# A new hand-written order for the start of a fused scan and feed-forward kernel

## The chip, the cores and the metric

The kernel runs on one core of one Trainium2 chip. The metric is the device time of one execution in microseconds. The median of three runs before the change is 116.46 us (116.0 to 116.67).

## What is computed

A state-space scan over x (4 batches, 8 heads, 768 steps, 32 channels) in chunks of 32 steps, with decays a and the projections B and C, is followed by a feed-forward layer with a squared ReLU.

```python
for c in range(nc):                                  # chunks of 32 steps
    cum = np.cumsum(la, axis=-1)                     # la = log(a)
    L = np.exp(cum[:, :, :, None] - cum[:, :, None, :]) * causal
    CB = np.einsum('bhin,bhjn->bhij', Cc, Bc)
    y_intra = np.einsum('bhij,bhjd->bhid', CB * L, xc)
    y_inter = np.einsum('bhin,bhnd->bhid', Cc, state) * decay_to_i
    y[:, :, sl] = y_intra + y_inter
    state = decay_full * state + np.sum(Bx, axis=2)  # Bx = B x, decayed to the chunk's end
...
h = np.maximum(x @ w_in, 0.0)                        # x: 3072 tokens of 256; w_in: 256 x 2048
out = (h * h @ w_out)                                # w_out: 2048 x 256
```

## The kernel before

The scan is cut into 12 units (`UNITS`: 4 batches by 3 thirds of 256 steps, the first third of all batches first). Each unit yields one block of 256 tokens for the feed-forward layer, so there are 12 blocks, a to l. TensorE does all products, ScalarE and VectorE take results out of PSUM, GpSimd prepares operands and issues the weight loads, SP issues most other loads.

Nothing is scheduled by the compiler: the string `ORDER` lists every step by a short name, and the loop over it emits the instructions of each step. Each engine then runs its own instructions in that order and waits at an instruction until what it needs is there. So the place of a name in the string sets the order on each engine and on each DMA queue.

The names, for unit or block k:

- `fa0`, `fa1`, `la`: loads of a (the two halves for the first third of the steps, then the rest); `ldC`, `ldB`, `ldx`: loads of a unit (`:l`/`:h` halves; the last letter is the queue: `a` ScalarE, `s` SP); `ld4` all three.
- `gB2`, `gB3`: a GpSimd memset of one column of the buffer that a load will fill, so that the load waits for GpSimd to get there (L134).
- `wi0` to `wi3`, `wo0` to `wo3`: loads of a quarter of w_in (L139) and of w_out (L143), issued by GpSimd, cast to bf16 on the way.
- `id3:512`: three matmuls on a constant (L476) that compute nothing that is used.
- `sk`, `sp`, `pk`, `su`, `to`, `fq`, `ps`, `iv`: the running product of a (L468, L469), its transposition by TensorE (L452), the totals (Ptot, L524) and their reciprocals and spread copies (Pinv, Pquad, P_sb). `sn`, `p2`, `pq`: the same for the later steps.
- `pc`, `pb`, `px`: C times the decay, the cast of B (both into jt), x over the decay (xs); `tr` and `tc`: transposition of jt by TensorE (L195) and the copy into bct. From unit 4 on the transposition is a DMA.
- `mt`: 16 matmuls that put a unit's scores into PSUM banks 0 to 3 (L220); `mk`: VectorE masks one bank straight from PSUM (L229, 0.68 us); `sc` with `ms`: ScalarE copies the bank out (L234) and VectorE or GpSimd masks the copy (L238).
- `u`: the unit's state update (16 matmuls); `sf`: the state times Pquad (Sd, L343); `in`, or its halves `ina` and `inb`: masked scores times xs (L245); `ca`: the carried state's part; `t`: the copy of the unit's result into T; `us`: the copy of its state out of PSUM.
- `a0` to `a7` (and so on to `l7`): up-projection of block a, eight parts, each four matmuls into one PSUM bank (L403) and a ReLU on ScalarE (L408); `qa0`: the square on VectorE (L414); `A0` to `A7`: the down-projection of that part, four matmuls that accumulate (L430).

Of the eight PSUM banks one is taken per up-projection in turn (`bank()`), from those that are not in use at that place of the order; a bank is free again where its reader stands in the order. A matmul into a bank waits for the bank's last reader. At most eight transfers of the ScalarE and SP queues are under way at a time: each waits for the one eight before it.

From `D0` on the order is a regular mixture of up- and down-projections, with the next units' steps between them.

Of the kernel before, what the change touches and what calls it, by code (L numbers as in the profile page):

```python
# [30 lines left out]
def kernel(  # L31
# [13 lines left out]
    nc = tc.nc  # L45
# [18 lines left out]
        g7 qg6 G3 mk8 h0 qg7 G4 pc10 pb10 px10 ld11 h1 qh0 G5 mk8 h2 qh1 G6 h3 qh2 G7 rg9 za9 zb9 sa9 sb9 h4 qh3 H0
        mk9 tr10 h5 qh4 H1 mk9 h6 qh5 H2 h7 qh6 H3 mk9 i0 qh7 H4 pc11 pb11 px11 i1 qi0 H5 mk9 i2 qi1 H6 i3 qi2 H7
        rg10 za10 zb10 sa10 sb10 i4 qi3 I0 mk10 tr11 i5 qi4 I1 mk10 i6 qi5 I2 i7 qi6 I3 mk10 j0 qi7 I4 j1 qj0 I5 mk10
        j2 qj1 I6 j3 qj2 I7 rg11 za11 zb11 sa11 sb11 j4 qj3 J0 mk11 j5 qj4 J1 mk11 j6 qj5 J2 j7 qj6 J3 mk11 k0 qj7 J4
        k1 qk0 J5 mk11 k2 qk1 J6 k3 qk2 J7 rg12 k4 qk3 K0 k5 qk4 K1 k6 qk5 K2 k7 qk6 K3 l0 qk7 K4 l1 ql0 K5 l2 ql1 K6
        l3 ql2 K7 l4 ql3 L0 l5 ql4 L1 l6 ql5 L2 l7 ql6 L3 ql7"""
# [694 lines left out]
```

## Time and profile before

| | |
|---|---|
| median of three runs | 116.46 us |
| the profiled execution | 116.84 us |
| its span, first to last instruction | 115.1 us |
| TensorE busy (matmuls) | 108.9 us |
| VectorE, ScalarE, GpSimd busy | 84.2, 76.7, 49.8 us |
| moved by DMA | 13.46 MB, 117 GB/s over the span |

The rows that the prediction shows come from these views. The first part of the page gives busy time, share and number of instructions of each engine. The chain that ended last is followed back from the last instruction, and its line gives each engine's share of it. A row of the costliest groups reads: line, engine, operation, what is written and read, sizes, count; then the total busy time, the mean of one in ns; then the idle time of that engine just before, and what ended it. A row of the timeline reads: start, duration, engine, line, operation, and in brackets the idle time before it and what ended it; rows with a count merge equal instructions that follow each other. A row of the windows reads: stretch, its length, then busy time of PE, PEld (weight loads), DVE (VectorE), ACT (ScalarE), POOL (GpSimd) with counts, the granted clock, the share of the DMA engines and GB/s. A row of the DMA issues ends with the size and the time from issue to landing.

### The profile page before, as it was taken

The numbers are of one execution on the slowest core, as the hardware profiler recorded it, in microseconds if no ns is written. First come the engines' busy times: TensorE is split into PE (matmuls) and PEld (weight loads), VectorE is DVE, ScalarE is ACT, GpSimd is POOL, SyncE is SP. The second block draws the span as 40 slices with busy tenths as digits, with TensorE's granted clock in tenths as the row PEclk, the third lists the DMA queues.
The fourth block names the chain that finished last, engine by engine and source line by source line (L and its number), as shares of the span: only waits on it lengthen the run. The fifth ranks groups of instructions, "written<-read, shape, count | busy, mean of one in ns | idle before, by whom it ended". The sixth has DMA issues, their size and how long they took to land.

```text
span 115.1 us, 3998 instructions
## 1 busy us (share of the span) xinstructions
PE 108.9 (95%) x1623; PEld 93.5 (81%) x1623; DVE 84.2 (73%) x187; ACT 76.7 (67%) x161; POOL 49.8 (43%) x102
## 2 busy tenths in 40 slices
PE   7977969999999999999999999999999999999990
PEld 2344749978898989989989989989989899899980
DVE  2469996779599969969965989849668488445530
ACT  0655667865598756787486686786777776876840
POOL 7369972068599457548602669038020020000000
PEclk9999999999999999999999999999999999999999
DMA  1999999989999913935915926623023020020202
GB/s 29 199 196 145 199 203 189 215 167 210 180 191 211 214 24 108 160 89 155 179 46 122 178 97 123 132 95 73 0 100 68 0 100 0 6 91 0 91 0 91
DMA packets 47814, 13.46 MB, mean 117 GB/s; under 512 B 44276, under 2 KB 45876, under 8 KB 47796
## 3 DMA queue, kind: packets, MB, share of 16 engines
q1 hardware_dynamic: 43828, 10.64, 44.8%
q0 software_dynamic: 1664, 2.10, 10.8%
q10 hardware_dynamic: 2304, 0.48, 2.0%
q8 instruction: 12, 0.20, 0.8%
q14 instruction: 6, 0.05, 0.1%
HBM read 10.58 MB, written 3.15 MB: 119 GB/s over the span
## 4 chain that ended last, share of the span: by engine, by line
PE 87%; DMA 6%; POOL 2%; issue 1%; DVE 1%; ACT 1%; ACTq 0%; DVEq 0%
PE pp L430 36%; PE pp L403 36%; PE pp L245 6%; DMA w_out_b<-in_moe_w_out_dram 6%; PE pp L476 4%; PE pp L220 3%; POOL mts L238 1%; PE pp L195 1%; POOL jt L158 1%; PE pp L452 1%; DVE jt L158 0%; DVE Sd L343 0%; ACT bct L208 0%; PE pp L521 0%; ACT osl L722 0%
## 5 line engine op out<-in xcount | busy, mean ns | idle before, releaser
L408 ACT ACTIVATE hb<-pp 128x512 bf16<-128x512 f32 x96 | 55.0, 599 | 24.7 <-PE pp L403 23.1
L430 PE MATMUL pp<-w_out_b,h 128*128 128x256 bf16 (+1 forms) x400 | 54.3, 268 | 0.8 <-DMA w_out_b<-in_moe_w_out_dram 0.8
L414 DVE TENSOR_TENSOR h<-hb 128x512 bf16<-128x512 bf16 x96 | 45.0, 486 | 12.7 <-ACT hb L408 12.3
L403 PE MATMUL pp<-T,w_in_b 128*128 128x256 bf16 x384 | 54.2, 273 | 0.0
L403 PEld LDWEIGHTS <-w_in_b 128*128 128x128 bf16 x384 | 41.4, 114 | 2.2 <-issue 1.0
L430 PEld LDWEIGHTS <-h 128*128 128x128 bf16 x400 | 37.6, 98 | 5.4 <-DVE T L210 1.1
L229 DVE TENSOR_TENSOR mts<-pp,mask 128x512 bf16<-128x512 f32 x45 | 29.6, 677 | 3.3 <-PE pp L220 3.3
L331 POOL TENSOR_TENSOR Sd<-z,Pquad 128x256 bf16<-128x256 f32 x16 | 11.1, 693 | 32.9 <-DVE z L315 25.7
L177 POOL TENSOR_TENSOR xs<-x_nat,Pinv 128x256 bf16<-128x256 f32 (+1 forms) x19 | 14.4, 776 | 5.2 <-DVE Pinv L546 4.6
L158 POOL TENSOR_TENSOR jt<-C_nat,P_sb 128x128 bf16<-128x128 f32 x22 | 9.4, 449 | 1.5 <-ACT P_sb L688 1.0
L476 PE MATMUL pp<-const-bfloat16-1.0 128*128 128x512 bf16 (+2 forms) x19 | 7.3, 516 | 0.8 <-PEq L748 0.8
L315 DVE SCALAR_TENSOR_TENSOR z<-z,Ptot,us 128x64 f32<-128x64 f32 x8 | 2.2, 281 | 6.3 <-ACT us L299 5.4
L437 ACT COPY osb<-pp 128x512 f32<-128x512 f32 x11 | 6.3, 584 | 0.4 <-PE pp L430 0.4
L245 PE MATMUL pp<-mts,xs 64*32 64x128 bf16 x384 | 5.9, 219 | 0.1
L170 POOL CAST jt<-B_nat 128x128 bf16<-128x128 f32 x17 | 5.4, 341 | 1.4 <-DMA B_nat<-in_B_dram 1.4
L220 PE MATMUL pp<-bct 32*64 32x256 bf16 x192 | 5.1, 279 | 0.9 <-DVE bct L210 0.6
L476 PEld LDWEIGHTS <-const-bfloat16-1.0 128*128 128x128 bf16 x19 | 2.2, 122 | 4.0 <-issue 3.7
L245 PEld LDWEIGHTS <-xs 64*32 64x32 bf16 x384 | 4.2, 90 | 0.6 <-issue 0.4
L282 ACT CAST T<-pp 128x512 bf16<-128x512 f32 x7 | 4.1, 592 | 0.4 <-PE pp L245 0.2
L208 ACT CAST T<-pp 128x256 bf16<-128x256 f32 x8 | 2.6, 375 | 2.6 <-PE pp L245 2.6
L245 PE MATMUL pp<-bct,Sd 128*128 128x128 bf16 x40 | 4.2, 220 | 0.0
L220 PEld LDWEIGHTS <-bct 32*64 32x64 bf16 x192 | 2.1, 102 | 2.0 <-issue 0.6
(62 smaller groups left out, 53.4 us busy)
## 6 DMA issues: line engine op xcount, KB each, us to landing
x_nat<-in_x_dram SPq DMA_DIRECT2D x11, 256.0 KB, 3.7
out_dram<-osb SPq DMA_DIRECT2D x11, 256.0 KB, 3.2
B_nat<-in_B_dram SPq DMA_DIRECT2D x11, 128.0 KB, 3.1
C_nat<-in_C_dram SPq DMA_DIRECT2D x11, 128.0 KB, 3.4
w_in_b<-in_moe_w_in_dram POOLq DMA_DIRECT2D x4, 256.0 KB, 6.8
w_out_b<-in_moe_w_out_dram POOLq DMA_DIRECT2D x4, 256.0 KB, 8.2
x_nat<-in_x_dram ACTq DMA_DIRECT2D x2, 128.0 KB, 3.4
bct<-jt SPq DMA_TRANSPOSE x8, 3.6
```

The lines of the kernel that those rows point to most:

```text
L158: eng.tensor_tensor(out=_fap(jt[k % 3], 128 + 144 * g, [[384, 2], [32, 4], [1, 16]]), in0=_fap(loaded[k]["C"], 128 * g, [[16, 2], [32, 4], ...
L177: eng.tensor_tensor(out=_fap(xs, 256 * r, [[256, 2 // n], [32, 8], [1, 32]]), in0=_fap(loaded[k]["x"], 32 * r, [[32, 2 // n], [64, 8], [1, ...
L220: nc.tensor.matmul(pp[64 * u:64 * u + 64, q, r * 256:r * 256 + 256], bct[32 * q:32 * q + 32, r, 0, u * 64:u * 64 + 64], _fap(bct[32 * q:32 ...
L229: nc.vector.tensor_tensor(out=live[k]["mts"][:, q].rearrange("p r g i -> p (r g i)"), in0=pp[:, q, :], in1=mask, op=ALU.mult)
L245: nc.tensor.matmul(dst, w, v, start=bool(need), stop=False, skip_group_check=True, **({} if pos is None else {"tile_position": pos}))
L331: nc.gpsimd.tensor_tensor(out=_fap(S_d, 0, [[128, 2], [32, 4], [1, 32]]), in0=_fap(z, 0, [[32, 2], [0, 4], [1, 32]]), in1=_fap(Pquad, 4 * ...
L403: nc.tensor.matmul(pp[:, h, i * 256:(i + 1) * 256], _fap(w, g * w.shape[2] + (o // 2) * 512 + 2 * (o % 2) + i, [[4, 128]]), T[blk][:, g].r ...
L408: nc.scalar.activation(out=hb.rearrange("p i t -> p (i t)"), in_=pp[:, h, :], func=AF.Relu)
L414: nc.vector.tensor_tensor(out=h2, in0=hb, in1=hb, op=ALU.mult)
L430: nc.tensor.matmul(dst, h2[:, i, r * 128:(r + 1) * 128], w_out_b[gi][:, 2 * o + i, c0:c1], start=first, stop=(fp == 7 and i == 1), skip_gr ...
L437: nc.scalar.copy(out=osb, in_=pp[:, 6 if blk == 1 else 7, :])
L476: nc.tensor.matmul(pp[:, h, 0:int(cols)], ones_b[:, 0:128], ones_b[:, 0:int(cols)] if dep is None else dep, start=True, stop=True, skip_gr ...
```

## The change

The first third of `ORDER` is rewritten up to `D0`, and from there it stays as it was. The pieces are the same but for these: GpSimd's first work is the constants that the start needs, then Pquad (`fq`), then one weight load after the other, with a mask (`ms0`), the scaling of unit 1's x (`px1`) and another mask (`ms1`) among them, and the gate of unit 2's B after the third w_in. Both halves of a are the first transfer of their queue, then come C, B and x of unit 0, then C, B and x of unit 1, then the rest of a. Some fillers go (19 matmuls become 18, eleven before the first product become six). Three quarters of unit 0's and unit 1's scores are masked straight from PSUM. C of unit 0 and of unit 1 is scaled on VectorE, half of unit 0's B is cast there, and one T half of units 0 and 1 is copied there. The state scaling of units 0 and 1 moves from VectorE to ScalarE, as four instructions. The up-projection `a0` stands ahead of the second scores `mt1`, and the down-projections of block a start before unit 1 is finished; blocks a, b and c follow in turn, each down-projection soon after its square. The totals for the later steps (`sn`, `p2`, `pq`) come some 50 names later.

```diff
     ORDER = """
-        id3:512 fa1:a la fa0:s ku ef ldx0:h:a eb id2:512 ti id1:512 gB3 pi ldB0:l:a hd ldC0:l:a ldB0:h:s ldC0:h:s
-        ldx0:l:a wm jz0:v mb jz1:v ldB1:s id3:512 sk pbh0:a id2:512 pk pbl0:p wi0 sp pc0:v ldC1:s trB0 wi1 su iv1:0:8
-        trC0 tcC0:0:v tcB0:2:a id1:512 tcC0:1:a ps pb1:a to px0:v jz2:v mt0 id1:512 u0:67 ldx1:s pc1:p fq sc0 mk0
-        id1:512 mk0 ms0:p tr1 tc1:1:v sc0 tc1:0:a sf0 mt1 ldB2:s wo0 ldC2:s ms0:v ldx2:s id1:384 in0 ca0 iv:8:16
-        id3:512 px1:p t0:aa id1:256 mk1 a0 a1 mk1 mk1 mk1 u1 ina1 inb1 sn1 us0 sf1 qa0 a3 ldC3:s wi2 fr p2 wi3 ca1
-        qa1 wo1 pc2 pb2:a t1:vv us1 iv:32:64 a2 zb0 qa2 zb1 A0 ldB3:s wo2 ldx3:s b3 qb3 b0 pq b2 b1 tr2 wo3 sb1 qa3
-        qb0 A1 b5 b4 qb1 qb2 qb5 tc2:1:v qb4 tc2:0:a a5 B0 b6 B1 a7 qa5 iv:16:32 px2 a6 mt2 B3 A2 sc2 u2 b7 us2 pb3:a
-        pc3 mk2 qa6 px3 mk2 A5 ms2:v mk2 ld4 qb6 sf2 a4 qa7 B5 pc4 A6 A3 ld5 pb4 ina2 inb2 tr4 ca2 t2:aa tr3 B4 B2
-        tc3:0:a tc3:1:a u3:45 qb7 ld6 ld7 mt3 qa4 B6 mk3 mk3 mk3 mk3 us3 c4 c5 c0 A4 A7 B7 c6 qc0 za3 qc4 c1 qc5 qc6
-        sa3 px4 qc1 pc5 pb5 bk c2 rg4 tr5 C0 mk4 mk4 qc2 c7 qc7 sb0 c3 qc3 d2 d1 C5 za4 afC2 d0 C1 px5 C4 qd2 zb3 C6
-        C3 qd0 d3 C2 mk4 mk4 C7 px6 sa4 rg5 qd3 sb3 pc6 zb4 sb4 pb6 D0 d4 qd1 tr6 mk5 za5 zb5 sa5 sb5 D1 iv:64:96 mk5
+        id3:512 fa1:a fa0:s ef jz0:v ldC0:l:a ldC0:h:s eb id2:512 ldB0:l:a ldB0:h:s hd ti ldx0:l:s ldx0:h:s ku pi
+        id1:512 sk wm mb jz1:v ldC1:s ldB1:s ldx1:s la sp id1:512 pk id1:256 pc0:v iv1:0:8 trC0 pbh0:a pbl0:v id1:384
+        tcC0:0:v tcC0:1:a trB0 su tcB0:2:a ps px0:v iv:8:16 to mt0 fr fq wi0 u0:67 id3:512 sc0 mk0 mk0 ms0:p sf0:a
+        mk0 pb1:a id1:512:0 ca0 ina0 id1:512 inb0 wo0 pc1:v t0:av px1:p id1:512 tr1 tc1:1:v tc1:0:a us0 id1:512 wi1
+        a0 mt1 mk1 sc1 mk1 a1 wo1 u1 qa0 ms1:p id2:512 ina1 mk1 A0 sf1:a qa1 inb1 ca1 t1:av A1 wi2 us1 iv:16:32 b0
+        gB2 ldC2:s ldB2:s ldx2:s wo2 jz2:v zb0 zb1 b1 a2 qb0 wi3 a3 qb1 wo3 B0 qa2 b2 B1 qa3 b3 qb2 A2 qb3 A3 sn1 B2
+        sb1 B3 a4 b4 qa4 a5 qb4 pc2 pb2:a gB3 ldC3:s ldB3:s ldx3:s ld4 ld5 b5 qa5 A4 qb5 tr2 tc2:1:v tc2:0:a B4 px2
+        p2 pq A5 iv:32:64 B5 a6 mt2 sc2 u2 us2 b6 mk2 qa6 mk2 a7 mk2 ms2:v qb6 sf2 b7 qa7 A6 qb7 ina2 inb2 B6 ca2
+        t2:aa pc3 pb3:a px3 pc4 pb4 tr4 A7 B7 c0 c1 qc0 tr3 tc3:0:a tc3:1:a c2 qc1 c3 qc2 u3:45 mt3 C0 mk3 qc3 C1 mk3
+        C2 mk3 us3 C3 mk3 za3 sa3 bk c4 c5 qc4 C4 px4 pc5 pb5 ld6 tr5 ld7 c6 qc5 C5 c7 qc6 rg4 mk4 C6 qc7 sb0 mk4 C7
+        zb3 sb3 za4 d0 sa4 px5 d1 mk4 qd0 d2 mk4 qd1 d3 px6 rg5 qd2 qd3 pc6 zb4 sb4 pb6 D0 d4 tr6 mk5 za5 zb5 sa5 sb5
+        D1 iv:64:96 mk5 d5 qd4 D2 pb7 d6 qd5 d7 qd6 D3 zb2 e0 qd7 mk5 e1 qe0 sb2 D4 mk5 D5 ld8 pc7 e2 qe1 D6 e3 qe2
...
-    def ph_sd_first(k):
+    def ph_sd_first(k, eng=None):
...
+        if eng is nc.scalar:
+            for q in range(4):
+                nc.scalar.activation(out=_fap(S_d, 32 * q, [[128, 2], [1, 32]]),
+                                     in_=_fap(pp, v["h"][0] * 512 + 256, [[32, 2], [1, 32]]),
+                                     func=AF.Copy, scale=Pquad[:, total(0, b, 0), q:q + 1])
+            v["S"] = [None, S_d]
+            return
```

More of the change, by code (lines that the diff above doesn't have):

```diff
@@ L64 @@
[L64 to L68, printed above, removed]
@@ L697, in one @@
                 "ms": lambda: mask_copied(k, eng),
-                "u": lambda: first_u(k, f[1] if len(f) > 1 else None), "sf": lambda: ph_sd_first(k),
+                "u": lambda: first_u(k, f[1] if len(f) > 1 else None), "sf": lambda: ph_sd_first(k, eng),
                 "ca": lambda: ph_carry(k, live[k]["h"], live[k]["begun"]),
```

14 lines of the change are left out of this document (9 added, 5 removed).

## The prediction

> **What bounds the kernel now.** I read the page first: busy shares, the chain that ended last, the costliest groups.
>
> ```profile
> span 115.1 us, 3998 instructions
> ...
> PE 108.9 (95%) x1623; PEld 93.5 (81%) x1623; DVE 84.2 (73%) x187; ACT 76.7 (67%) x161; POOL 49.8 (43%) x102
> ...
> PE 87%; DMA 6%; POOL 2%; issue 1%; DVE 1%; ACT 1%; ACTq 0%; DVEq 0%
> ...
> L408 ACT ACTIVATE hb<-pp 128x512 bf16<-128x512 f32 x96 | 55.0, 599 | 24.7 <-PE pp L403 23.1
> ...
> L414 DVE TENSOR_TENSOR h<-hb 128x512 bf16<-128x512 bf16 x96 | 45.0, 486 | 12.7 <-ACT hb L408 12.3
> L403 PE MATMUL pp<-T,w_in_b 128*128 128x256 bf16 x384 | 54.2, 273 | 0.0
> ...
> L229 DVE TENSOR_TENSOR mts<-pp,mask 128x512 bf16<-128x512 f32 x45 | 29.6, 677 | 3.3 <-PE pp L220 3.3
> L331 POOL TENSOR_TENSOR Sd<-z,Pquad 128x256 bf16<-128x256 f32 x16 | 11.1, 693 | 32.9 <-DVE z L315 25.7
> L177 POOL TENSOR_TENSOR xs<-x_nat,Pinv 128x256 bf16<-128x256 f32 (+1 forms) x19 | 14.4, 776 | 5.2 <-DVE Pinv L546 4.6
> ```
>
> TensorE carries 87% of the chain; once its stream is dense, only a stop of TensorE moves the end. So I read its timeline for where the stream starts and stops, and then the windows with the stops.
>
> ```profile
> 0.85 4.85 PE L476 MATMUL pp<-const-bfloat16-1.0 128*128 128x512 bf16 x11 [0.85 <-PEq L748]
> 5.63 0.64 PE L452 MATMUL pp<-eye_f,cp 64*64 64x32 f32 x8
> ...
> 8.09 0.42 PE L220 MATMUL pp<-bct 32*64 32x256 bf16 x16 [0.24 <-ACT bct L208]
> ...
> 11.44 0.93 PE L476 MATMUL pp<-const-bfloat16-1.0 128*128 128x512 bf16 x4
> 12.20 1.03 PE L403 MATMUL pp<-T,w_in_b 128*128 128x256 bf16 x8
> ...
> 16.96 0.60 PE L430 MATMUL pp<-w_out_b,h 128*128 128x256 bf16 x4 [0.81 <-DMA w_out_b<-in_moe_w_out_dram]
> 17.39 1.91 PE L403 MATMUL pp<-T,w_in_b 128*128 128x256 bf16 x16
> ```
>
> ```profile
> 14.00:15.00 1.00, 0.82 (x12) 0.49 (x10) 0.96 (x3) 0.61 (x2) 0.98 (x4) 1.00 1.05 195
> 15.00:16.00 1.00, 0.91 (x8) 0.76 (x8) 1.00 (x5) 0.54 (x5) 0.76 (x2) 1.00 1.22 215
> 16.00:17.00 1.00, 0.19 (x3) 0.07 (x2) 1.00 (x4) 0.53 (x4) 0.73 (x2) 1.00 1.22 198
> ...
> 26.00:28.00 2.00, 1.89 (x22) 1.56 (x25) 2.00 (x4) 1.33 (x5) 1.77 (x3) 1.00 1.09 209
> ```
>
> The stream of useful work begins with a0 at 12.20. After that the windows show 0.18 + 0.09 + 0.81 + 0.11 = 1.2 us of idle in four stops, and none worth counting later. Sixteen matmuls lie 1.91 us from first start to last end while one lasts 0.273, so they start 0.109 apart and each record runs 0.16 beyond the next possible start: a stop costs its idle plus 0.16, and the four cost 1.8 us. A group of four (one a0, one A0) is 0.44.
>
> **The start.** Here are the rows that set it.
>
> ```profile
> a_nat<-in_a_dram ACTq DMA_DIRECT2D x1, 16.0 KB, 1.6
> ...
> B_nat<-in_B_dram SPq DMA_DIRECT2D x1, 64.0 KB, 3.1
> ...
> a_nat<-in_a_dram SPq DMA_DIRECT2D x1, 16.0 KB, 3.0
> ```
>
> ```profile
> 4.68 0.22 DVE L468 TENSOR_SCALAR a_cl<-a_nat 64x128 f32<-64x128 f32 x1 [0.99 <-DMA a_nat<-in_a_dram]
> ...
> 11.00 2.42 DVE L229 TENSOR_TENSOR mts<-pp,mask 128x512 bf16<-128x512 f32 x4
> ...
> 18.72 1.14 DVE L414 TENSOR_TENSOR h<-hb 128x512 bf16<-128x512 bf16 x3 [0.57 <-ACT hb L408]
> ```
>
> ```profile
> 8.44 0.18 ACT L524 COPY Ptot<-pp 128x8 f32<-128x8 f32 x1
> ...
> 11.43 0.65 ACT L208 CAST T<-pp 128x256 bf16<-128x256 f32 x2 [1.41 <-PE pp L245]
> ...
> 13.81 0.28 ACT L296 COPY us<-pp 128x128 f32<-128x128 f32 x1
> ...
> 18.09 2.06 ACT L408 ACTIVATE hb<-pp 128x512 bf16<-128x512 f32 x4 [0.59 <-PE pp L403]
> ...
> 26.32 0.51 ACT L168 CAST jt<-B_nat 128x128 bf16<-128x128 f32 x2
> ...
> 29.04 0.88 ACT L208 COPY bct<-pp 128x384 bf16<-128x384 bf16 x2
> ...
> 33.16 1.08 ACT L437 COPY osb<-pp 128x512 f32<-128x512 f32 x2 [0.17 <-PE pp L430]
> ```
>
> ```profile
> 5.61 1.64 POOL L139 DMA_DIRECT2D w_in_b<-in_moe_w_in_dram  x2 [0.17 <-issue]
> ...
> 9.24 1.15 POOL L238 TENSOR_TENSOR mts<-sc,mask 128x512 bf16<-128x512 bf16 x1
> ```
>
> Today half of a is issued second on SP, takes 3.0 us, and the scan starts at 4.68. Issued first on each queue both halves should take the 1.6 us of ACT's, so a is there at 2.4. The matmuls on cp (5.63 now) then wait only for the six fillers left: 0.85 + 6 x 0.43 (4.85 less the 0.16 tail, over eleven) = 3.4. Carrying the same intervals on, the first scores move from 8.09 to about 6.2, Ptot from 8.44 to 6.2, the last mask of unit 0 (three at 0.61 on VectorE, the fourth 1.15 on GpSimd beside them) to 8.7, and T0 is ready at 9.6 instead of 12.08. Two operations are new: VectorE's cast of half of B (64 elements) lies between nothing and the 0.36 from square to square of 512, I take 0.2; ScalarE's Sd is four instructions of 128x64, bounded by the 0.18 and 0.28 of the copies above, I take 0.6 for the four. Both end before the mask they stand beside.
>
> The weights pay for this. Now the first w_in is issued at 5.61; in the new order it stands behind Pquad, hence behind Ptot: 6.6.
>
> ```profile
> w_in_b<-in_moe_w_in_dram POOLq DMA_DIRECT2D x1, 256.0 KB, 5.5
> ...
> w_out_b<-in_moe_w_out_dram POOLq DMA_DIRECT2D x1, 256.0 KB, 6.5
> ...
> C_nat<-in_C_dram SPq DMA_DIRECT2D x1, 128.0 KB, 13.7
> ```
>
> At 5.5 us to landing, a0 starts at 12.1. But now x, B and C are on the queues beside it; in the new order SP's next big load waits for GpSimd's gate gB2, eight microseconds later, so the transfer should be quicker; 3.1 us, what a 64 KB load of B takes now, is out of reach for four times the bytes. I take 4.6: a0 at 11.2, **1.0 us earlier** (0.1 to 1.4). T0, ready at 9.6, waits. Against it, 0.35 (second scores) and 0.44 (two fillers) that lay ahead of a0 now lie behind it: **+0.8**.
>
> **The dense part.** This is where I expect the loss. The old order keeps a reserve of A and B down-projections whose squares are long done and puts them wherever another product is late. The new order spends each at once, and puts consumers directly behind producers. An up-projection to its down-projection needs 0.60 on ScalarE and 0.42 on VectorE; a score to its use needs 0.68 on VectorE. I walked all five queues of the new order with the durations above (0.49 from one full-bank copy of ScalarE to the next: 2.06 less the last one's 0.60, over three; likewise 0.36 between squares and 0.61 between masks), in order on each engine. "Behind" means queued behind on that engine. TensorE stops at:
>
> - a1, which needs the bank that the first mask of unit 1 frees: 0.16 + 0.68 behind mt1's last matmul, **0.9**; u1, inb1 (behind the four ScalarE instructions of sf1) and b0 (behind T1): **0.1 + 0.35 + 0.25**;
> - tr2, behind pb2, which stands behind three ReLUs on ScalarE: **0.5**;
> - u2 and b6, whose banks the ReLU of a6 and the score copy free: **0.7**;
> - in2: VectorE has after mt2 three masks, a mask from SBUF, two squares and sf2, 3 x 0.61 + 4 x 0.36 = 3.3 us; TensorE has u2, b6, a7, b7, A6, 1.9, plus the 0.7 above: **0.75**;
> - tr3 to mt3: behind T2 ScalarE queues two casts of B, two output copies, four ReLUs and two bct copies, 0.65 + 0.41 + 0.95 + 4 x 0.49 + 0.77 = 4.7 us; TensorE has c0 to c3, ca2, tr3 and u3, 2.4 us, and little else left of A and B: **1.5** in four stops;
> - C4, directly behind c5: its square is behind four masks of unit 3: **0.95**; C7, behind c7 and a mask of unit 4: **0.75**;
> - region 5, behind two Sd and two xs on GpSimd (2 x 0.69 + 2 x 0.78): **1.1**.
>
> Together **7.8 us**, where the old order's rows show 1.8. The same walk on the old order finds only 1.0 of those 1.8 (late weights and slow squares are missing in it), so I add 0.7 for what it misses again. Sum: -1.0 + 0.8 + 7.8 - 1.8 + 0.7 = **+6.5 us**. Against its own execution that is a span of 121.6 for 115.1; that execution took 116.84 in all, 1.74 around the span, and stands 0.38 above the median of the runs. On the median: 116.46 + 6.5 = **122.9 us**. All later blocks have the same order in both and keep their spacing; their work hides nothing, as TensorE is solid there.
>
> Bounds: if every transfer were early, a0 follows T0 and the later stops absorb most of it: about +5.5; if squares and masks also overlap better than I queue them and a third of the stops goes, +3.5. Upwards: w_in at 5.5 and w_out at 6.5 us (issued 8.5, there at 15.0, A0 walked at 14.0) cost up to 1.2. B of unit 2 is issued behind gB2 at 14.6 with four weight transfers after it; the C load above took 13.7 us under four weights, and by that ScalarE would stand at pb2 until the weights are through, about 24.4 instead of 23.3: +1.2. Both: +8.9.
>
> **A rule on the clock.** Eleven fillers take 0.43 us each and the four at 11.44 take 0.93 together, 0.22 apart: TensorE runs at half speed at first, though the granted clock in the windows reads 1.00. [...] Six fillers are 2.6 us. The trace agrees that fillers speed up, after 4.85 us of them.
>
> **Rivals.** *Slow clock until the dense part (about 16 us).* The fillers' 0.43 against 0.22 doubles the 3 us of matmuls between a0 and there and the small ones before T0; part hides in the stops: +2.8 more, 125.7. For: half as many fillers and gaps between them; against: transposes, sums and scores follow without a gap of more than 0.6 us. [...]
>
> *The early start holds and the stops don't come.* If squares and masks keep ahead of TensorE, the order wins: -1.0 + 0.8 - 1.8 + 0.7 = -1.3, 115.1. It decides at C4: for it speaks that VectorE is only 73% busy; against, its windows at 14 to 17 and 26 to 28 are full already in the old order. If only a third of the stops come, the loss is 7.8 / 3 - 1.3 = +1.3, 117.8.
>
> *Starved loads.* Weights from GpSimd back to back take the DMA from x, B and C of units 2 and 3 until after 24.4; then +8.9, 125.4, as above. [...]
>
> **How the numbers follow.** Forecast (+3.5 to +8) 0.67; starved loads 0.08; slow clock 0.08; a third of the stops 0.06; gain 0.07; no net change (gain and stops equal) 0.04. Predicted time 122.9. The range 119.6 to 125.4 leaves out the gain, most of the third and the slow clock's far end. About 0.5% is what a measurement of this kernel can tell from none: faster 0.07, same 0.04, slower 0.89.
>
> **What would show it.** Right: cp's matmuls at 3.4; a0 near 11.2 behind a DMA; then VectorE and ScalarE named as releasers of TensorE's stops between 11 and 48, 9 us or so in all; A6 and B7 done before T2; equal spacing after 60. Wrong: a0 behind T0; fillers still at 0.43 after 6; TensorE at nine tenths or more in every slice from 12 us on; or ScalarE standing at pb2 behind B.

## The result, and the profile after

The changed kernel takes 127.4 us (median of four runs, 126.07 to 127.8); the kernel before took 116.56 beside it (116.0 to 117.21). The ratio is 1.091, with a 95% interval of 1.081 to 1.101: slower by 10.8 us, where 6.5 was forecast. Here and below, a ratio leaves out runs more than 1.5% above their kernel's fastest, so it can lie below that of the medians. The profiled execution took 127.12 us with a span of 125.4, where the prediction's walk has 121.6. The sign and most of the reasons were right, the size was not, and 127.4 lies above the range.

From the page of the kernel after: span, busy shares, the granted clock over the span, the engines' shares of the chain, and the costliest groups.

```profile
span 125.4 us, 4000 instructions
...
PE 113.8 (91%) x1622; PEld 94.0 (75%) x1622; DVE 84.7 (68%) x187; ACT 79.3 (63%) x170; POOL 49.4 (39%) x100
...
PEclk9999558999999999999999999999999999999999
...
PE 76%; DVE 8%; ACT 4%; DMA 4%; issue 3%; POOL 2%; ACTq 0%
...
L410 PE MATMUL pp<-T,w_in_b 128*128 128x256 bf16 x384 | 55.1, 275 | 3.1 <-DMA w_in_b<-in_moe_w_in_dram 1.9
L437 PE MATMUL pp<-w_out_b,h 128*128 128x256 bf16 (+1 forms) x400 | 55.1, 270 | 1.7 <-DVE h L421 1.7
...
L229 DVE TENSOR_TENSOR mts<-pp,mask 128x512 bf16<-128x512 f32 x45 | 29.9, 678 | 6.4 <-PE pp L220 6.4
```

Three things differ. TensorE's share of the chain fell from 87% to 76%, and VectorE took 8%. The down-projections (L437) now wait for squares (h, L421), 1.7 us. And the clock row has two fives: for two of the forty slices TensorE ran at half speed, which the kernel before did not do in its profile. The other runs of the changed kernel have it too. One step at half (they are 3.41 us long, as the windows below show) takes 3.41 x 0.5 / 125 = 0.014 off a run's mean clock; the four runs read 0.972, 0.986, 0.959 and 0.970, so two, one, three and two such steps, at spans of 125.4, 124.4, 126.1 and 126.0 us.

The start, from the timeline of the kernel after (start, duration, instruction; in brackets the wait and what ended it):

```profile
3.62 0.64 PE L459 MATMUL pp<-eye_f,cp 64*64 64x32 f32 x8
...
6.41 0.42 PE L220 MATMUL pp<-bct 32*64 32x256 bf16 x16
...
10.19 0.38 PE L483 MATMUL pp<-const-bfloat16-1.0 128*128 128x512 bf16 x1
12.44 0.94 PE L410 MATMUL pp<-T,w_in_b 128*128 128x256 bf16 x4 [1.86 <-DMA w_in_b<-in_moe_w_in_dram]
...
14.82 1.01 PE L410 MATMUL pp<-T,w_in_b 128*128 128x256 bf16 x4 [0.86 <-DVE mts L229]
15.76 0.31 PE L245 MATMUL pp<-xs,jt 64*32 64x64 bf16 x16
15.99 1.04 PE L483 MATMUL pp<-const-bfloat16-1.0 128*128 128x512 bf16 x2
...
17.51 1.04 PE L437 MATMUL pp<-w_out_b,h 128*128 128x256 bf16 x4
...
20.05 1.94 PE L410 MATMUL pp<-T,w_in_b 128*128 128x256 bf16 x16
```

Up to 10 us it runs nearly as walked (3.62 and 6.41 where 3.4 and 6.2 were forecast). Then w_in lands 5.3 us after its issue at 7.05, and a0 starts at 12.44, not 11.2. From there matmuls take double: four up-projections 0.94 and 1.01 instead of 0.60, two fillers 1.04. The last row is b0, at full clock again. The windows, cut where the clock changes (length, TensorE's busy time, granted clock, share of the DMA engines, GB/s), show the half clock:

```profile
9.20:12.62 3.42, 1.56 (x27) 1.00 1.08 148
12.62:16.03 3.41, 2.55 (x41) 0.50 0.83 113
16.03:19.44 3.41, 3.36 (x49) 0.50 0.84 117
19.44:22.86 3.42, 3.31 (x29) 1.00 1.09 179
```

The stops of the dense part, from the same timeline:

```profile
28.19 0.51 PE L195 MATMUL pp<-eye_b,jt 128*128 128x128 bf16 x6 [0.29 <-ACT jt L168]
...
31.86 0.25 PE L245 MATMUL pp<-xs,jt 64*32 64x64 bf16 x16 [0.33 <-ACT hb L415]
32.34 1.72 PE L410 MATMUL pp<-T,w_in_b 128*128 128x256 bf16 x12 [0.22 <-ACT sc L234]
...
35.05 0.47 PE L245 MATMUL pp<-mts,xs 64*32 64x128 bf16 x32 [0.57 <-DVE Sd L350]
...
40.24 0.26 PE L220 MATMUL pp<-bct 32*64 32x256 bf16 x1 [0.24 <-ACT hb L415]
40.73 0.42 PE L220 MATMUL pp<-bct 32*64 32x256 bf16 x14 [0.22 <-ACT hb L415]
...
44.96 0.61 PE L437 MATMUL pp<-w_out_b,h 128*128 128x256 bf16 x4 [1.03 <-DVE h L421]
...
49.05 0.61 PE L437 MATMUL pp<-w_out_b,h 128*128 128x256 bf16 x4 [0.65 <-DVE h L421]
...
51.81 0.27 PE L245 MATMUL pp<-bct,Sd 128*128 128x128 bf16 x2 [0.22 <-ACT hb L415]
52.47 0.22 PE L245 MATMUL pp<-xs,jt 64*32 64x64 bf16 x8 [0.24 <-POOL xs L177]
```

Each is a product right behind its producer, with ScalarE or VectorE as the releaser, and GpSimd for the last.

To place the loss, count TensorE's work: each matmul, fillers left out, with its mean spacing after 55 us in the kernel before (0.1095 for a weight matmul, 0.066 for 128x128, 0.022 for a score, 0.012 and 0.005 for the two forms of the sums; the few f32 ones 0.03 to 0.1 by their rows). The table has when the kernel before has 12, 18, ... us of this work behind it, and how much later each other kernel is there (e1 and so on are the experiments below).

```
work done, us       12     18     22     26     30     60
before, at       23.50  30.08  34.05  38.19  42.28  72.60
after            +3.68  +5.71  +7.26  +8.42 +10.22 +10.28
e1               +2.73  +4.78  +6.32  +7.49  +9.27  +9.33
e2               +0.48  +3.38  +4.92  +6.09  +7.89  +7.95
e3               +4.09  +6.12  +7.26  +7.89  +9.23  +9.28
e4               +0.27  +0.49  +0.49  +0.49  +0.49  +0.49
e6               +0.95  +2.26  +3.40  +4.03  +5.38  +5.44
e9               -0.02  -0.02  -0.02  -0.02  -0.02  -0.02
e12              +3.10  +5.33  +6.88  +8.05  +9.83  +9.89
e13              +2.73  +4.77  +6.31  +7.48  +9.27  +9.33
e14              +0.42  +2.31  +3.86  +5.03  +6.84  +6.90
```

The kernel after is 3.7 us late when the dense part begins, loses 6.5 more up to 30 us of work, and nothing behind that; 10.3 is also the difference of the two spans. The split at 12 us is good to about half a microsecond, since it moves by as much with the sizes taken for the f32 products; the differences between after, e2 and e14 in that column don't move with them.

### The profile page after: what moved, and what is told of

Its sections match the earlier page's. It is cut to its first block, busy times and chain, and to the rows that moved or that the text cites. A ratio compares the mean times of both kernels' runs of the same rounds, so it can differ in the third digit from the quotient of the medians.

```text
span 125.4 us, 4000 instructions
## 1 busy us (share of the span) xinstructions
PE 113.8 (91%) x1622; PEld 94.0 (75%) x1622; DVE 84.7 (68%) x187; ACT 79.3 (63%) x170; POOL 49.4 (39%) x100
## 3 DMA queue, kind: packets, MB, share of 16 engines
q1 hardware_dynamic: 44884, 10.90, 45.6%
## 4 chain that ended last, share of the span: by engine, by line
PE 76%; DVE 8%; ACT 4%; DMA 4%; issue 3%; POOL 2%; ACTq 0%
PE pp L437 30%; PE pp L410 30%; PE pp L245 6%; DVE mts L229 5%; DMA w_in_b<-in_moe_w_in_dram 4%; PE pp L483 4%; PE pp L220 4%; DVE h L421 2%; ACT hb L415 1%; POOL xs L177 1%; PE pp L195 1%; PE pp L459 1%; ACT jt L168 1%; ACT Sd L345 1%; ACT bct L208 1%
## 5 line engine op out<-in xcount | busy, mean ns | idle before, releaser
L421 DVE TENSOR_TENSOR h<-hb 128x512 bf16<-128x512 bf16 x96 | 46.8, 503 | 17.8 <-ACT hb L415 17.4
L410 PE MATMUL pp<-T,w_in_b 128*128 128x256 bf16 x384 | 55.1, 275 | 3.1 <-DMA w_in_b<-in_moe_w_in_dram 1.9
L437 PE MATMUL pp<-w_out_b,h 128*128 128x256 bf16 (+1 forms) x400 | 55.1, 270 | 1.7 <-DVE h L421 1.7
L437 PEld LDWEIGHTS <-h 128*128 128x128 bf16 x400 | 37.3, 99 | 7.3 <-DVE h L421 2.7
L331 POOL TENSOR_TENSOR Sd<-z,Pquad 128x256 bf16<-128x256 f32 x16 | 10.3, 648 | 34.2 <-DVE z L315 22.9
L245 PE MATMUL pp<-mts,xs 64*32 64x128 bf16 x384 | 6.8, 226 | 0.6 <-DVE Sd L350 0.6
L220 PE MATMUL pp<-bct 32*64 32x256 bf16 x192 | 5.8, 291 | 0.7 <-ACT hb L415 0.5
L208 ACT CAST T<-pp 128x256 bf16<-128x256 f32 x10 | 3.4, 374 | 2.9 <-PE pp L245 2.8
L170 POOL CAST jt<-B_nat 128x128 bf16<-128x128 f32 x16 | 4.8, 329 | 0.0
L245 PE MATMUL pp<-xs,jt 64*32 64x64 bf16 x160 | 3.4, 199 | 0.9 <-ACT hb L415 0.3
L245 PEld LDWEIGHTS <-Sd 128*128 128x128 bf16 x40 | 3.1, 98 | 1.4 <-ACT Sd L345 0.6
```

The source lines that it names most:

```text
L220: nc.tensor.matmul(pp[64 * u:64 * u + 64, q, r * 256:r * 256 + 256], bct[32 * q:32 * q + 32, r, 0, u * 64:u * 64 + 64], _fap(bct[32 * q:32 ...
L245: nc.tensor.matmul(dst, w, v, start=bool(need), stop=False, skip_group_check=True, **({} if pos is None else {"tile_position": pos}))
L331: nc.gpsimd.tensor_tensor(out=_fap(S_d, 0, [[128, 2], [32, 4], [1, 32]]), in0=_fap(z, 0, [[32, 2], [0, 4], [1, 32]]), in1=_fap(Pquad, 4 * ...
L410: nc.tensor.matmul(pp[:, h, i * 256:(i + 1) * 256], _fap(w, g * w.shape[2] + (o // 2) * 512 + 2 * (o % 2) + i, [[4, 128]]), T[blk][:, g].r ...
L421: nc.vector.tensor_tensor(out=h2, in0=hb, in1=hb, op=ALU.mult)
L437: nc.tensor.matmul(dst, h2[:, i, r * 128:(r + 1) * 128], w_out_b[gi][:, 2 * o + i, c0:c1], start=first, stop=(fp == 7 and i == 1), skip_gr ...
```

## The experiments

The times are medians of four to twelve runs, with the lowest and the highest in brackets. Diffs show the pieces of `ORDER` that differ.

**e1, fillers in the idle ahead of a0.**

```diff
-us0 id1:512 wi1 a0
+us0 id9:512 wi1 a0
```

> The kernel after, with nine filler matmuls instead of one ahead of a0, where TensorE stood idle from 10.4 to 12.44 us; nothing else differs. Theory (the idle behind the late w_in drops TensorE's clock to half): the granted clock stays 1.00 from 12 to 20 us, the four matmuls of a0 take 0.44 instead of 0.94, b0 starts at 17.2 to 17.6 instead of 20.05, and the time is 127.4 - 2.7 = 124.7 us. Rival (the sparse stretch from 12 to 20 drops the clock whatever lies ahead of it, since its stops are as long): granted clock 0.5 for some 6.8 us again, 127.2 to 127.7. Rival (the half clock hides in the stops that are there anyway): clock 1.00 but the time within 0.7 us of 127.4.

126.21 us (125.09 to 126.93). In its profile the clock was halved once, but earlier, and not behind the fillers (windows and timeline):

```profile
4.14:7.55 3.41, 2.36 (x43) 1.00 1.20 181
7.55:10.96 3.41, 3.37 (x39) 0.50 1.07 155
10.96:14.38 3.42, 3.35 (x35) 1.00 0.87 106
```

```profile
13.41 0.60 PE L411 MATMUL pp<-T,w_in_b 128*128 128x256 bf16 x4
...
16.87 0.61 PE L438 MATMUL pp<-w_out_b,h 128*128 128x256 bf16 x4
...
19.09 1.94 PE L411 MATMUL pp<-T,w_in_b 128*128 128x256 bf16 x16
```

The order up to 10 us is that of the kernel after; only the steps of the clock lie elsewhere, and what stands between 7.55 and 10.96 ran at half speed. w_in landed at 13.06 (issued at 7.16, 5.9 us on the way), 0.7 later than in the kernel after, and the fillers, still running then, put a0 off to 13.41. From a0 (first row) to b0 (last) it is 5.68 us, where the kernel after has 20.05 - 12.44 = 7.61: the half clock costs **1.9 us** between these two points. The gain foreseen is there in this stretch, the time foreseen is not. The other three runs read a mean clock of 1.00 and took 125.09 to 126.93, still above the 124.7 foreseen.

**e2 and e14, the first w_in issued early** (the same kernel twice).

```diff
-fr fq wi0 u0:67
+fr fq u0:67
...
-ku pi id1:512 sk
+ku pi wi0 id1:512 sk
```

> The kernel after, with the issue of the first w_in moved back ahead of the second set of fillers (issue near 4 us instead of 7.05); nothing else differs. Theory (weight issue late, clock behind it): w_in lands by 9.5, a0 starts behind T0 at 9.8 to 10.3 instead of 12.44, no idle of TensorE over 1 us, granted clock 1.00, b0 at 15.0 to 15.8; time 127.4 - 2.3 - 2.6 = 122.5 us. Rival (the clock falls in the sparse stretch anyway): a0 at 10, but clock 0.5 for 6.8 us, time 125 to 126. Rival (only the stops count, the start is absorbed by them): a0 at 10, time 126.5 to 127.5.

124.55 us (124.03 to 125.16) and, again, 124.27 (123.76 to 125.05). The clock stays at 1.00 in both profiles; a0 starts at 10.96 and 11.11. From e14, two windows, a0 and b0, and a cast on ScalarE:

```profile
7.32:10.74 3.42, 2.65 (x44) 1.00 1.06 183
10.74:14.15 3.41, 2.55 (x49) 1.00 0.73 117
```

```profile
11.11 0.60 PE L411 MATMUL pp<-T,w_in_b 128*128 128x256 bf16 x4
...
16.79 1.94 PE L411 MATMUL pp<-T,w_in_b 128*128 128x256 bf16 x16
...
9.99 0.50 ACT L169 CAST jt<-B_nat 128x128 bf16<-128x128 f32 x2 [1.74 <-DMA B_nat<-in_B_dram]
```

In the table the start's loss shrinks from 3.7 to 0.5 and 0.4: the late w_in and the clock behind it cost 3.2 to 3.3 us together. The time fell by 2.9 and 3.1, less than the 4.9 expected, since b0 (16.86 and 16.79) lies a good microsecond behind the time foreseen. Most of that is at a0, and the cast shows why: with w_in issued at 3.44, beside the load of unit 1's B (issued at 3.92), that B is there at 9.99 in e14, where the kernel after has it at 7.88. (In e2, e9 and e13, with the early weight, it lands at 9.8 to 10.2, in e1 and e3, with the late one, at 8.0.) ScalarE waits 1.74 us for it, and half of T0 and the transposes of unit 1 stand behind that cast. So the early weight was paid for by the next unit's load, and a0 came 1.3 to 1.5 us earlier instead of 2.1 to 2.6. The dense part loses what it did, and in e2 one stop of 0.62 more (a mask of unit 2).

**e13, the fillers taken out of that kernel.**

```diff
-id3:512 sc0
+sc0
...
-pb1:a id1:512:0 ca0 ina0 id1:512 inb0
+pb1:a ca0 ina0 inb0
...
-px1:p id1:512 tr1
+px1:p tr1
...
-us0 id1:512 wi1 a0
+us0 wi1 a0
```

> The kernel after with early w_in (124.55, clock 1.00 in its profile, a0 to b0 5.9 us), without its seven 512-column fillers between the second scores of unit 0 and a0; nothing else differs. Theory (too little work of the array in a stretch of 3.4 us halves the clock, whatever makes it little): a stretch after 6 us falls below 1 us of full-array work, the granted clock is 0.5 for 3.4 or 6.8 us directly behind it, a0 to b0 takes 7.3 to 7.7, time 125.5 to 127. Rival (the late loads, not the idle array, halve it): clock 1.00, a0 to b0 5.9, time 124 to 124.6, or less, as the fillers stand in the way.

> The kernel after with early w_in once more, beside the kernel without fillers: theory 124.0 to 125.2 with the clock at 1.00 from 6 us on; if the clock is halved here as well, the comparison of the two doesn't tell what halves it.

126.11 us (125.67 to 126.91) against 124.27. The windows without the fillers:

```profile
4.75:8.17 3.42, 1.81 (x42) 1.00 1.03 151
8.17:11.58 3.41, 1.94 (x41) 0.50 1.11 191
11.58:14.99 3.41, 2.55 (x41) 0.50 0.61 93
14.99:18.41 3.42, 3.37 (x56) 0.50 1.11 166
18.41:21.82 3.41, 3.29 (x29) 1.00 1.08 169
```

```profile
11.39 1.06 PE L411 MATMUL pp<-T,w_in_b 128*128 128x256 bf16 x4
...
19.10 1.94 PE L411 MATMUL pp<-T,w_in_b 128*128 128x256 bf16 x16
```

Useless matmuls taken away make the kernel slower by 1.8 us: the clock is at half for 10.2 us, and from a0 at 11.39 to b0 at 19.10 it is 7.71 us, where the kernel with fillers needs 5.68. w_in is issued early in both, and lands within 0.4 us of the same time. So what halves the clock here is too little work of the array, not the late load; the load was one way to get there. Three of the four runs read a mean clock of 0.956 to 0.959, three steps at half; with the fillers one of four has a single one (0.986). But the fourth run without fillers reads 1.00 and is the slowest, 126.91. As the time before the first rise counts as 1.00, its clock may have come up late, as in e12; only its time is on record, and this stays open. TensorE was never idle for long: its waits in the first of these windows and over its end were 0.67 and 1.11 us, and the longest up to b0 is 1.15.

**e12, fillers in both sparse stretches of the kernel after.**

```diff
-to mt0 fr fq wi0 u0:67 id3:512
+to id1:512 mt0 fr fq wi0 id1:512 u0:67 id4:512
...
-us0 id1:512 wi1 a0
+us0 id9:512 wi1 a0
```

> The kernel after with three fillers more between 6 and 8 us and eight more ahead of a0; w_in stays late, the dense order stays. Theory (late w_in costs by itself 1.2, and through the clock some 2 more): granted clock 1.00 from 6 us to the end, no L484 filler over 0.3 us apart after 6 us, a0 at 12.4 to 13, time 127.4 - 2.2 = 125.2 at most, spread below 1.5. Rival (the clock falls all the same, since the stretch from 12 to 17 us is sparse): 126.2 to 127.5 as with the eight fillers alone.

126.89 us (126.45 to 127.22). From 9.80 us on the clock is full, and a0 to b0 is 5.68 again (13.79 to 19.47). But in this execution the clock first came up at 9.80, not at 5.8, everything before ran late, and the fillers pushed a0 back: w_in was there at 12.6. Fillers behind a late load can't win more than the load lets through; the time expected was missed.

**e4, the late w_in alone, in the old order.**

```diff
-pk pbl0:p wi0 sp
+pk pbl0:p sp
...
-fq sc0 mk0 id1:512
+fq wi0 sc0 mk0 id1:512
```

> The kernel before, with the issue of the first w_in alone moved behind Pinv (the second w_in keeps its place); nothing else differs. Theory (late first weights leave TensorE idle, and that drops the clock): a0 at 13.3 to 13.7 instead of 12.2, an idle of 1 us or more ahead of it, granted clock 0.5 for some 6.8 us from there, time 116.5 + 1.3 + 2.6 = 120.4. Rival (lateness alone): clock 1.00, time 117.5 to 117.9. Rival (the reserve of the old order takes it up): 116.3 to 117.0.

118.07 us, ratio 1.019 (1.009 to 1.029), between the 120.4 of the theory and the 117.9 of lateness alone:

```profile
13.92 0.30 PE L404 MATMUL pp<-T,w_in_b 128*128 128x256 bf16 x1 [1.22 <-DMA w_in_b<-in_moe_w_in_dram]
```

a0 is 1.7 us later, TensorE was idle for 1.22, the clock stayed, and the table has only 0.27 to 0.49 left of it: in its profile the old order's reserve takes up most of the delay. That is the fastest of its four runs. One more, at 117.62, kept the clock; the other two read a mean of 0.983, about one step at half, and took 118.52 and 119.01. So in the old order too a late w_in can cost the clock, in some executions.

**e3, two stops of the dense part taken apart.**

```diff
-tr4 A7 B7 c0 c1 qc0 tr3
+tr4 c0 c1 qc0 tr3
...
-u3:45 mt3 C0
+u3:45 A7 B7 mt3 C0
...
-c4 c5 qc4 C4 px4 pc5 pb5 ld6 tr5 ld7 c6 qc5 C5 c7 qc6 rg4 mk4 C6
+c4 c5 qc4 px4 pc5 pb5 ld6 tr5 ld7 c6 qc5 C4 c7 qc6 rg4 mk4 C5 C6
```

> The kernel after, with the two last products of units 0 and 1 (A7, B7) kept as a reserve for the stop ahead of mt3, and C4 put one up-projection further behind its own (ahead of rg4 instead of behind c5), C5 beside C6; nothing else differs. Theory (each stop of TensorE is a product put directly behind its producer): the stops at mt3 (0.24 + 0.22) and at C4 (1.03) go for the most part, 1.1 to 1.3 us in all, time 126.2. Rival (the stop goes to the next consumer, since VectorE is the bound there): the idle of TensorE between 39 and 54 us stays 2.5 us or more in sum, time 127.0 to 127.5. The clock from 12 to 20 us is untouched in both.

125.41 us (123.94 to 126.85). C4 and C7 in its timeline:

```profile
44.84 0.61 PE L438 MATMUL pp<-w_out_b,h 128*128 128x256 bf16 x4 [0.53 <-DVE h L422]
48.06 0.61 PE L438 MATMUL pp<-w_out_b,h 128*128 128x256 bf16 x4 [0.22 <-DVE h L422]
```

The waits fell from 1.03 and 0.65 to 0.53 and 0.22, those ahead of mt3 went, and a new one of 0.46 came (for T of unit 2). The dense part loses 9.28 - 4.09 = 5.2 us instead of 6.6: 1.4, about as expected. The times spread with the clock at the start: two runs at a mean of 0.973, the profiled one among them, took 126.14 and 126.85, the two at 1.00 and 0.986 took 124.67 and 123.94.

**e6, the same, early w_in, and the queues of ScalarE and VectorE reordered.**

```diff
-a4 b4 qa4
+a4 pc2 pb2:a b4 qa4
...
-A5 iv:32:64 B5 a6 mt2 sc2 u2 us2 b6 mk2 qa6 mk2 a7 mk2 ms2:v qb6 sf2 b7 qa7 A6 qb7 ina2 inb2 B6
+iv:32:64 a6 mt2 sc2 A5 u2 us2 b6 mk2 mk2 mk2 qa6 a7 ms2:v sf2 B5 qb6 b7 A6 qa7 ina2 inb2 qb7 B6
```

> The kernel after with four edits: the first w_in early and the two spacings of C4, A7 and B7 (both as run alone), and new here, between a4 and in2, the masks of unit 2 ahead of the squares of a6 and a7, the casts of B of unit 2 two ReLUs earlier, and A5, B5 behind the scores they are to cover. Theory (the stops between 25 and 54 us are products directly behind their producers, and ScalarE's and VectorE's queue order sets them): the new edits take 1.2 to 1.6 us beyond the sum of the two known ones (124.55 - 1.4), time 121.7 us. Rival (VectorE and ScalarE are the bound there, so stops only move): the idle of TensorE from 25 to 54 us falls by less than 1.8 us in all, time 123.2 to 124.2.

122.28 us (122.2 to 122.91), 0.6 above the theory and below the rival. The dense part's loss is 5.44 - 0.95 = 4.5 us, where the kernel after has 6.6. The wait for Sd fell from 0.57 to 0.26, those at tr2 and u2 are gone. So stops go when products stand further behind their producers; what is left shows where this order has no reserve.

**e9, the new start and the old dense order.** The start of the kernel after with both first weights early, and from a1 on the kernel before:

```diff
-ku pi id1:512 sk
+ku gB3 pi wi0 id1:512 sk
...
-mk0 ms0:p sf0:a mk0
+mk0 ms0:p wi1 sf0:a mk0
...
-us0 id1:512 wi1 a0 mt1 mk1 sc1 mk1 a1 wo1 u1 qa0 ms1:p
+id1:512 a0 mt1 jz2:v ldB2:s ldC2:s ldx2:s mk1 a1 mk1 mk1 mk1 u1 ina1 inb1 sn1 us0 sf1 qa0 a3 ldC3:s wi2 p2 wi3
```

> The start of the kernel after up to the second scores (loads, three masks from PSUM, T0 ahead of unit 1), with its first w_in early and its second behind the mask on GpSimd, and from a1 on the order of the kernel before, with its reserve of down-projections; B of unit 1 is cast ahead of its transposes. Theory (the 7 us and more between 25 and 54 us come from the new dense order alone): no stop of TensorE over 0.5 us after 20 us, time 116 to 117.5, within 1% of the kernel before, and 7 to 8 us below the kernel after with early w_in (124.55). Rival (the new start hands late loads or late squares to the dense part, and the stops come from there): 119 us or more, with stops over 0.5 us after 20 us. In both the clock may be halved once in the sparse stretch ahead of 16 us, which costs up to 2.

116.91 us, ratio 1.007 (1.003 to 1.011). From the windows of this kernel:

```profile
22.00:24.00 2.00, 2.00 (x33) 1.00 1.16 207
...
32.00:36.00 4.00, 4.00 (x96) 1.00 1.12 201
...
44.00:48.00 4.00, 4.00 (x39) 1.00 0.89 140
```

TensorE is solid from 20 us on (0.1 us idle up to 52), and in the table the kernel is level with the one before. With the new loads, the three masks from PSUM and T0 ahead of unit 1, but the old dense order, the loss becomes none; against e14, which has the first weight early too, that is 6.9 us. The early start gains nothing either: T0 is ready at 10.90 instead of 12.08 and a0 at 11.25 is 0.95 earlier than before, but three waits around it take that back:

```profile
10.69 0.51 PE L196 MATMUL pp<-eye_b,jt 128*128 128x128 bf16 x6 [0.69 <-ACT jt L169]
13.06 0.60 PE L404 MATMUL pp<-T,w_in_b 128*128 128x256 bf16 x4 [0.86 <-DVE mts L230]
14.26 0.24 PE L246 MATMUL pp<-xs,jt 64*32 64x64 bf16 x12 [0.39 <-DVE mts L230]
```

They are the scan of unit 1 (its B, then its masks), which starts later than it did: its transposes are at 10.69, in the kernel before at 9.18. As in e14, its B lands at 10.1, beside the early weight. Of the twelve runs, four with one step at half (mean clock 0.985) took 117.55 to 118.48, the other eight 116.60 to 117.27.

**e5, a first form of this.** Here the second w_in stands behind C of unit 1, and the transposes of unit 1 run ahead of the cast of its B, so that unit 1 computes without its B.

```diff
-trC0 tcC0:0:v tcC0:1:a trB0 su tcB0:2:a ps px0:v iv:8:16 to mt0 fr fq wi0 u0:67
+trC0 tcC0:0:v tcC0:1:a trB0 su tcB0:2:a ps to px0:v jz2:v mt0 id1:512 u0:67 pc1:p wi1 fq sc0
...
+mk0 ms0:p tr1 tc1:1:v sc0 tc1:0:a sf0 pb1:a mt1
```

> The kernel before from the first up-projection of unit 0 on (its order of up- and down-projections and its reserve), behind the loads and the first scan of the kernel after, with the first w_in issued ahead of the second set of fillers and the second w_in behind C of unit 1. Theory (the loss of the kernel after lies in its late first weights and in its order of the dense part, while a first is worth having): a0 at 10.3 to 11 instead of 12.2, no stop of TensorE over 0.5 us between 20 and 52 us, time 116.6 - 1.5 = 115.1 us. Rival (the loads first are themselves a cost, since weights and later B, C and x land later): 117 to 118.5. Rival (the early start is absorbed by the squares, which set the pace until 20 us): 116.2 to 117.

117.99 us (115.6 to 120.37), ratio 1.001 (0.995 to 1.007): neither the gain of the theory nor a clear loss. In its profile the clock was at half from 9.10 to 15.92 us.

**e7, e10 and e11, loads and fillers.** e7 is the kernel before with the new order of the first loads alone, e11 adds five fillers to it between 6 and 11 us, e10 adds three to e9.

```diff
-id3:512 fa1:a la fa0:s ku ef ldx0:h:a eb id2:512 ti id1:512 gB3 pi ldB0:l:a hd ldC0:l:a ldB0:h:s ldC0:h:s ldx0:l:a wm
+id3:512 fa1:a fa0:s ef ldC0:l:a ldC0:h:s eb id2:512 ldB0:l:a ldB0:h:s hd ti ldx0:l:s ldx0:h:s ku la id1:512 gB3 pi wm
```

The fillers of e11, and those of e10:

```diff
-trB0 wi1 su
+trB0 id2:512 wi1 su
...
-id1:512 tcC0:1:a
+id2:512 tcC0:1:a
...
-mt0 id1:512 u0:67
+mt0 id2:512 u0:67
...
-ms0:p tr1
+ms0:p id1:512 tr1
```

```diff
-to mt0 fr fq u0:67 id3:512
+to id1:512 mt0 fr fq id1:512 u0:67 id4:512
```

> The kernel before with the new order of the first loads alone: a first on both queues, then C, B, x; weights, masks and all later work at their old places. Theory (T0 comes up to 2 us earlier, but the first w_in then sets a0): T0 ready by 11, a0 at 11.0 to 11.6 instead of 12.2, time 115.5 to 116.1. Rival (w_in gets later too, as four loads now lie ahead of it and beside it): a0 at 12 to 13 behind w_in, time 116.5 to 117.5. Rival (loads are hidden anyway): 116.4 to 116.9.

> The kernel of the run beside it, with three filler matmuls of 512 columns more between 6 and 8 us, where TensorE waits. Theory (the clock is halved after a stretch of 3.4 us in which the array works less than about a third of what it could; ten profiles show it after windows of 0.55 to 1.08 us of full-array work, not after 1.19 or more): those windows rise by 0.64 us, no granted clock of 0.5 before the last 3 us of the profile, and the spread of the times is below 1.5 us. Rival (the clock falls by something else): 0.5 shows again in the profile or the times spread over 2.5 us as those of the kernel before with the new loads did (115.9 to 119.0).

> The kernel before with the new order of the first loads (as run alone: 115.9 to 119.0 in two groups, clock halved from 9.8 to 16.6 us in its profile), with five filler matmuls more between 6 and 11 us, where TensorE waits. Theory (low work in one window of 3.4 us halves the clock in some executions): the upper group (117.4 to 119) goes, times 115.8 to 116.8, clock 1.00 in the profile. Rival (the two groups come from the loads, that is from when C and B land): two groups as before, the clock notwithstanding.

e7: 117.43 us (115.91 to 119.0), ratio 1.002 (0.997 to 1.007), no gain. Its profile is of the slowest run: the clock is halved from 9.78 to 16.60, and a0 is at 14.62. e11: 116.70 (115.6 to 120.09), clock 1.00 from its rise at 6.3 us on in its profile, but the upper times are still there, so the fillers didn't do what the theory said of them. The kernel before itself ranges from 115.27 to 119.06 in 28 runs beside e7. Its 64 runs beside the experiments tell a part of why: six with two or three steps at half (mean clock 0.971 and less) took 117.63 to 119.06, 53 without a whole one 115.27 to 118.93, with a median of 116.5. What makes the upper times of those stays open. e10: 117.52 (116.54 to 118.09); in its profile the clock is never halved between its first rise and the kernel's end (one of the other five runs reads 0.985), the spread is 1.55 us where 1.5 was the bound, and it came up late, at 9.80, as in e12. The early loads alone (e7) are worth nothing that can be measured here.

**e8, three masks from PSUM in the old order.**

```diff
-tc1:1:v sc0 tc1:0:a
+tc1:1:v mk0 tc1:0:a
...
-ldC2:s ms0:v ldx2:s
+ldC2:s ldx2:s
```

> The kernel before with unit 0's third mask taken from PSUM by VectorE (0.61) instead of a copy to SBUF by ScalarE (0.49) and a mask from there (0.36); nothing else differs. Theory (VectorE sets T0): a0 0.2 to 0.4 later, time 116.8 to 117.0. Rival (the copy was on the path): a0 0.1 to 0.3 earlier, 116.3 to 116.5.

116.27 us, ratio 0.999 (0.995 to 1.003): no difference that can be told. In its profile a0 is at 12.55, 0.35 later, as the theory has it; the time it gave is not. None of the kernels tried is measurably faster than the one before.

## Why the prediction was wrong, step by step

**The sign and the dense part: right.** The steps from tr2 to region 5 have 6.25 us, 6.95 with the 0.7 for what the walk misses, if that is put here. The table has 10.22 - 3.68 = 6.5. Stop by stop (idle time plus 0.16): tr2 0.45 (0.5 forecast), u2 and b6 0.87 (0.7), in2 0.73 (0.75), C4 1.19 (0.95), C7 0.81 (0.75), region 5 0.78 (1.1). The stops ahead of mt3 were fewer, two of about 0.5 each, from one score's start to the next, for 1.5. Together these are 5.8. The places were all foreseen; that the sum is so near owes something to luck, as sizes too large and too small partly cancel. That the order is the cause is shown by e9, in which the old order has none of it behind the new start, and by e3 and e6, which take 1.4 and 2.1 us of it away by spacing.

**The start: wrong by 4.1 us, and this is the step that failed.** By the prediction's terms the kernel should have entered the dense part 0.4 us early: -1.0 and +0.8 at a0, 1.6 us of stops up to b0, less the old order's 1.8. It was 3.7 late. (With the 0.7 put to the start instead, the error is 3.4.) Three terms make this up:

- *The clock, 1.9 us, left out of the sum.* The forecast ran everything after the fillers at full speed. It carried the half clock only as a rival with a chance of 0.08, and that rival in another form: a clock that does not come up before the dense part. It came up at 5.8, before the 6 that the prediction set, and fell back at 12.6. How often it falls changes from run to run, one to three steps in the four runs, so a part of this size is chance. The rival was weighed by gaps ("gaps between them" for it, "without a gap of more than 0.6 us" against it). That gaps decide was the author's estimate, which no row of before shows, and it is a wrong measure: e13 falls after waits of 0.67 and 1.11 us, e4 keeps the clock after one of 1.22. By work it would have looked otherwise: the prediction's own walk has T0 ready at 9.6 and a0 waiting for w_in until 11.2, a stretch of 1.6 us with little for TensorE but six transposes and two fillers.
- *The landing of w_in, 1.24 us.* 4.6 us were taken and 5.3 measured, with the issue at 7.05 instead of 6.6; the upper bound given for a0, 12.1, was nearly the truth.
- *The stretch from a0 to b0 at full clock, some 0.8 us.* With w_in early and the clock full, e14 enters the dense part at +0.4 instead of -0.4, and A0 starts at 14.74, where the walk had 14.0. The new Sd on ScalarE takes 0.93 for four instructions, where 0.6 was assumed:

```profile
7.44 0.93 ACT L345 ACTIVATE Sd<-pp,Pquad 128x64 bf16<-128x64 f32 x4
```

For the rest, e14's timeline gives an estimate: a0 to A0 takes 3.63 there and 2.8 in the walk. The largest piece, 0.3, lies between the sums of unit 1 (14.23) and A0 (14.74), since 16 sums at a spacing of 0.012 take 0.2; 0.16 lies behind u1, and the other pieces, where one kind of product follows another, are 0.1 and less. The walk counts each group at its steady spacing and has nothing for these changes. No run tried them one by one.

Together 3.9 of the 4.1 us. The first two are firm: e14, without them, is 3.26 us less late. The third hangs on the split of the table at 12 us, good to half a microsecond.

**The rivals.** The early start without stops (115.1) and a third of the stops (117.8) fell with the dense part's 6.5 us. Starved loads, in the form of this rival, are not the cause: GpSimd waits 4.6 us for x of unit 2 in the kernel after, but the stop at tr2, which stands behind the cast of B, is 0.29, and ScalarE's casts of that B (27.63) follow a ReLU without a wait:

```profile
27.39 1.25 POOL L177 TENSOR_TENSOR xs<-x_nat,Pinv 128x512 bf16<-128x512 f32 x1 [4.58 <-DMA x_nat<-in_x_dram]
```

The slow clock had the right cost, matmuls that take double (0.94 us for a0's four, 0.60 at full clock), at the wrong place, and its 2.8 us stand beside the measured 1.9. Had that rival been carried as a term, with w_in at its upper bound, the sum would have been 6.5 + 0.9 + 2.8 = 10.2 with the prediction's own price, which is 126.7, and 9.3 or 125.8 with the measured one; 127.4 came.

**The range.** It ended at 125.4 because its upper end adds the two bounds on loads (6.5 + 1.2 + 1.2 = 8.9) and leaves the clock out. But the late load and the half clock come together, as the load that is late makes the stretch that is sparse. (Its lower end, 119.6, does not follow from the +3.5 given for it, which is 120.0.)

## What to carry to other kernels

An early start pays only if the next thing in the chain is early as well: here unit 1's scan and the first weights were not. A load brought forward can put off the one beside it: with the first weight early, the B of unit 1 was there at 9.99 instead of 7.88 (e14), and T0 earlier by 1.2 us bought nothing (e9). A reserve of work whose inputs are long done is what keeps a full engine full; spending it at once costs the sum of all producer-to-consumer distances, which a walk over the queues found here to half a microsecond, stop by stop and in sum. And when loads move, look at what TensorE does meanwhile: fillers that compute nothing were worth 1.8 us (e14 against e13), and after a stretch with little work even the useful matmuls took double (four of a0 0.94 us in the kernel after, 0.60 in e14).

## What the runs showed of the hardware

In the 16 profiles of this case the granted clock changed only at steps of 3.41 us, whose phase differs from run to run: it first came up at 3.9 (e14) to 9.8 us (e10, e12). (Before that the rows read 1.00, though fillers start 0.43 us apart, twice the 0.22 of later ones.) What decides seems to be the array's work in the step before. Count one for a matmul on 128 rows and 128 columns of the array with 512 columns of data (a filler; at 0.219 us apart some 15.6 of them fill a step), smaller ones by their share of rows, columns and data, f32 like bf16. This is the author's count, not a reading of the profile. Of the 519 steps from the first rise on, these are the ones at full clock with the least work. Eight more, each the last step of its kernel, are left out; they have 1.75 to 5.00, and half follows in all.

```
work in fillers   the step after it
2.52  e5          half
3.27  e13         half
4.00  e3          half
4.02  e1          half
4.52  e7          half
4.75  e2          full
5.00  after       half
5.02  e6          half
5.14  e4, e8      full
5.25  e9          full
5.38  e10         full
more              full, in all
```

So a third of what the array can do, 5.14 of 15.6 and more, kept the clock in every step, 4.52 and less lost it in every one, and between lie both. Waits alone don't lose it: e4 idles 1.22 us and keeps it. The kernel after falls with 5.00. TensorE's busy time doesn't sort the steps: those that lost the clock have 1.39 to 2.46 us of it, and e2 keeps the clock with 2.17. The bound is a pattern drawn from the 16 profiles that it sorts, not a measured threshold; the experiment behind it is e13 against e14. Why the clock came up only at 9.80 in e10 and e12, though TensorE was busy for all of the step from 2.98 to 6.39, stays open.
